# Making the sign words of split weights with a multiply by 0.0 in place of a comparison

## The chip, the cores and the metric

The kernel runs on one core of one Trainium2 chip. The metric is the device time of one execution in microseconds (us), lower is better. Engines are named as the profile names them: PE is TensorE (PEld its weight loads), DVE is VectorE, ACT is ScalarE, POOL is GpSimd, SP issues most of the DMAs.

## What is computed

Causal attention (4 batches, 8 heads, 576 positions, head size 64) with a bias made from running sums of `s`, followed by two dense layers on the 2304 rows of width 512. Each layer goes up to 2048 and back; the first gates with `relu6`, the second with a sigmoid. The weights arrive as 64-bit floating-point numbers.

```python
scores = scale * q @ k.T + min(-(cum[i] - cum[j]), 0), causal
x = softmax(scores) @ v
h = x @ w_in;  x = (h * clip(h + 3, 0, 6) / 6) @ w_out
h = x @ w2_in; out = (h * sigmoid(h)) @ w2_out
```

Only the way in which a weight's 64-bit words become a 32-bit number is touched by the change.

## The kernel before

**Stages.** Up to about 40 us only attention runs, with matmuls on a constant tile (`keep_clock`) between. Up to about 525 us each slot of the program does one head's attention and one step of the first dense layer (`slot`): the step multiplies the weights of one or two chunks with a block of 256 tokens (`first`, L260 to L262), gates the product (`gate_high`: ScalarE L272, VectorE L273, high half `gh` copied on GpSimd by L114), makes the rest `gl` (`gate_low`, VectorE L280), and multiplies by the second weights (`second`, L299 to L301). Every number is carried as a high and a low half, so each product takes three matmuls. Up to about 620 us the last block of 512 tokens runs while the weights of the second layer are prepared, the layer's input is split (`split2`, ScalarE L1033, VectorE L1034 and L1038, names `x1b`, `x1t`, `xr`), and the second layer begins. From there on the second layer has the core to itself (`product` L1068 to L1070, `sums2` L1085 to L1087); the last chunk of weights is prepared before 700 us.

**The feed of weights.** There are 64 chunks of 128 x 512 weights, 16 for each of the four matrices: `i` (up) and `o` (down), for two layers. A chunk goes through `load` (a DMA of 512 KB into a tile `rawi` or `rawo` of 128 x 1024 words, L147), `fields`, `join`, and then, for all but the second layer's up weights, `high` and `low`; those up weights go into sums of a faster product scheme instead (`Two`, L970, L980, L982). In a loaded tile a number's low word and high word lie side by side, so `low` and `high` are every second word of it:

```python
nc.scalar.activation(low, low.bitcast(U32), AF.Copy, scale=2.0**-29)
nc.scalar.activation(f32(self.mag), f32(high), AF.Abs, scale=2.0**-112)
```

The first line (L159) leaves the low word's top three bits as an integer. The second (L160) reads the high word as a 32-bit float and leaves its magnitude, with the exponent moved, in a tile `mag`. L161, on GpSimd, overwrites the high word by its sign alone. `join` on VectorE shifts `mag` left by three and ors the sign word in (L172, two SBUF inputs of integers), then adds the low bits (L176). ScalarE makes the high half of the result (L120), VectorE the low half (L187).

**What sets the order.** `Feed.tick` calls these steps for successive chunks, one chunk a step behind the other; `mag` has three buffers, so L160 of a chunk waits until the chunk three places ahead has been split. The code calls the engines in one order, and then the tile context is opened with `schedule_with_timeline_sim=True`: a planner that holds a duration for every instruction rearranges each engine's stream. A change of an instruction's kind therefore changes the order of others. Within an engine instructions run strictly in that order.

Of the kernel before, what the change touches and what calls it, by code (L numbers as in the profile page):

```python
# [14 lines left out]
ALU = mybir.AluOpType  # L15
# [1 line left out]

P = 128
BIG = 3e38
SIGN = -(2**31)  # L20


def f32(ap):
    return ap.bitcast(F32)
# [3 lines left out]
def kernel(  # L28
# [59 lines left out]
    def heads_of(x):  # L88
# [8 lines left out]
        out=cmask[:, NZ:], in_=cmask[:, NZ:], pattern=[[-1, P]],  # L97
# [32 lines left out]
    class Chunk:  # L130
# [20 lines left out]
        def fields(self):  # L151

            self.mag = stage.tile([P, DM], I32, tag="mag", name=f"mag{self.nm}")
            if self.src.dtype == F32:
                nc.scalar.copy(f32(self.mag), self.val)
                self.val = f32(self.mag)
                return
            low, high = self.words
            nc.scalar.activation(low, low.bitcast(U32), AF.Copy, scale=2.0**-29)  # L159
            nc.scalar.activation(f32(self.mag), f32(high), AF.Abs, scale=2.0**-112)  # L160
            nc.gpsimd.tensor_scalar(  # L161
                out=high, in0=f32(high), scalar1=0.0, scalar2=float(SIGN),
                op0=ALU.is_lt, op1=ALU.mult,
            )

        def join(self):
# [164 lines left out]
    def bank(kind, shape, name):  # L331
# [11 lines left out]
        out=srow, in0=srow, scalar1=0.0, scalar2=1.0 / SCALE, op0=ALU.max, op1=ALU.mult  # L343
# [944 lines left out]
```

## Time and profile before

| what | us |
| --- | --- |
| median of 3 runs | 1000.9 |
| lowest of the runs | 996.92 |
| the profiled execution's own time | 1001.75 |
| its span, first to last instruction | 1000.0 |
| mean granted TensorE clock in it | 0.995 of full |

The rows further down are from that one profiled execution. One of the three runs took 1356.65 us and stands apart from the others. A busy time is the sum over an engine's instructions; a wait is an engine's idle time just before an instruction, put down to what ended it. Times in timelines count from the first instruction.

### The profile page before, as it was taken

What the parts mean: (1) busy time and instruction counts of PE and PEld (TensorE: products, weight loads), DVE (VectorE), ACT (ScalarE), POOL (GpSimd) and SP (SyncE); (2) the same over time, 40 slices, a digit from 0 to 9 for tenths busy, and PEclk for the clock granted to TensorE, in tenths of its full rate; (3) what the DMA queues carried; (4) which work ended last, traced back from release to release, by engine and by line L of the source; (5) the groups of instructions that cost most, each with busy time, mean ns of one, the idle gap of its engine ahead of it and who ended that gap; (6) DMA issues with size and microseconds to landing.
All of it is one profiled execution on the core that took longest, in us unless ns stands there. A gap on an engine that the chain in (4) does not pass through costs nothing.

```text
span 1000.0 us, 17975 instructions
## 1 busy us (share of the span) xinstructions
PE 976.2 (98%) x6292; PEld 895.8 (90%) x6292; DVE 738.4 (74%) x1757; ACT 510.9 (51%) x1177; POOL 311.3 (31%) x323
## 2 busy tenths in 40 slices
PE   8998999999999999999999999999999999999997
PEld 5787989999999999999997877798988989889996
DVE  6898999888789888988877889887574434743343
ACT  6898555554555555555546566564443323432332
POOL 4456743433233443433425465532000000000000
PEclk9999999999999999999999999999999999999999
DMA  5786212312222223213215967434354243442421
GB/s 177 238 273 197 60 34 74 91 44 64 85 69 82 69 57 88 69 53 91 58 31 181 380 239 235 165 117 189 121 205 170 74 147 104 170 156 76 147 74 64
DMA packets 54419, 125.41 MB, mean 125 GB/s; under 512 B 12332, under 2 KB 34076, under 8 KB 51000
## 3 DMA queue, kind: packets, MB, share of 16 engines
q1 hardware_dynamic: 53880, 123.60, 37.3%
q8 instruction: 50, 0.82, 0.3%
q10 hardware_dynamic: 448, 0.66, 0.2%
q14 instruction: 41, 0.34, 0.1%
HBM read 99.52 MB, written 24.69 MB: 124 GB/s over the span
## 4 chain that ended last, share of the span: by engine, by line
PE 75%; DVE 11%; DMA 5%; POOL 3%; issue 2%; ACT 2%; SPq 1%; POOLq 0%; DVEq 0%; ACTq 0%
PE a L1085 6%; PE a L1086 6%; PE a L1087 6%; PE h L1068 5%; PE h L1070 5%; PE h L1069 5%; PE ph L260 5%; PE ph L261 5%; PE ph L262 5%; PE acc L300 4%; PE acc L299 4%; PE acc L301 4%; PE poB L672 4%; POOL rawo L161 2%; PE pt0B L580 1%
## 5 line engine op out<-in xcount | busy, mean ns | idle before, releaser
L300 PE MATMUL acc<-gl,wo 128*128 128x256 f32 (+1 forms) x512 | 152.9, 300 | 3.4 <-DVE gl L280 3.4
L260 PE MATMUL ph<-xh,wi 128*128 128x256 f32 (+1 forms) x512 | 152.9, 300 | 2.5 <-DVE g L273 1.9
L301 PE MATMUL acc<-gh,wo 128*128 128x256 f32 (+1 forms) x512 | 151.5, 297 | 0.0
L261 PE MATMUL ph<-xl,wi 128*128 128x256 f32 (+1 forms) x512 | 150.6, 294 | 0.0
L262 PE MATMUL ph<-xh,wi 128*128 128x256 f32 (+1 forms) x512 | 150.4, 294 | 0.0
L299 PE MATMUL acc<-gh,wo 128*128 128x256 f32 (+1 forms) x512 | 145.3, 300 | 0.0
L1127 ACT ACTIVATE gh<-h 128x384 fp32r<-128x384 f32 x96 | 50.3, 524 | 185.4 <-DVE h L1135 185.3
L1085 PE MATMUL a<-wo,gh 128*128 128x512 f32 x288 | 113.5, 394 | 1.4 <-ACT gh L1127 0.9
L1086 PE MATMUL a<-wo,gh 128*128 128x512 f32 x288 | 113.1, 393 | 0.0
L300 PEld LDWEIGHTS acc<-gl,wo 128*128 128x128 f32 x512 | 98.1, 192 | 8.1 <-DVE gl L280 5.2
L260 PEld LDWEIGHTS ph<-xh,wi 128*128 128x128 f32 x512 | 96.3, 188 | 7.7 <-DVE g L273 3.3
L301 PEld LDWEIGHTS acc<-gh,wo 128*128 128x128 f32 x512 | 98.1, 192 | 3.2
L299 PEld LDWEIGHTS acc<-gh,wo 128*128 128x128 f32 x512 | 96.8, 191 | 3.4
L261 PEld LDWEIGHTS ph<-xl,wi 128*128 128x128 f32 x512 | 96.4, 188 | 3.2
L262 PEld LDWEIGHTS ph<-xh,wi 128*128 128x128 f32 x512 | 96.5, 188 | 3.1
L161 POOL TENSOR_SCALAR rawi<-rawi 128x512 int32<-128x512 f32 x32 | 69.5, 2173 | 80.2 <-ACT magi L160 53.3
L1087 PE MATMUL a<-wo,gl 128*128 128x512 f32 x288 | 90.0, 392 | 0.0
L161 POOL TENSOR_SCALAR rawo<-rawo 128x512 int32<-128x512 f32 x32 | 72.2, 2258 | 49.7 <-ACT mago L160 40.9
L1129 DVE TENSOR_TENSOR gl<-h,gh 128x384 fp32r<-128x384 f32 x96 | 53.8, 560 | 39.8 <-ACT h L1128 38.0
L1135 DVE TENSOR_TENSOR h<-h,u 128x384 f32<-128x384 f32 x72 | 40.1, 557 | 53.5 <-PE h L1070 53.2
L114 POOL TENSOR_SCALAR gh<-g 128x512 fp32r<-128x512 f32 x68 | 49.8, 734 | 88.7 <-DVE g L273 79.6
L1068 PE MATMUL h<-x0t,w 128*128 128x384 f32 x192 | 64.9, 338 | 0.7 <-DVE u L1135 0.7
(221 smaller groups left out, 2564.9 us busy)
## 6 DMA issues: line engine op xcount, KB each, us to landing
w<-w_d SPq DMA_DIRECT2D x18, 1792.0 KB
w_d<-w SPq DMA_DIRECT2D x8, 1792.0 KB
k2B<-in_kT_dram SPq DMA_DIRECT2D x64, 144.0 KB
rawi<-in_w1i_dram SPq DMA_DIRECT2D x16, 512.0 KB
rawo<-in_w1o_dram SPq DMA_DIRECT2D x16, 512.0 KB
rawi<-in_w2i_dram SPq DMA_DIRECT2D x16, 512.0 KB
rawo<-in_w2o_dram SPq DMA_DIRECT2D x16, 512.0 KB
q2B<-in_qT_dram SPq DMA_DIRECT2D x64, 80.0 KB
```

The costliest lines, as they stand in the source:

```text
L161: nc.gpsimd.tensor_scalar(out=high, in0=f32(high), scalar1=0.0, scalar2=float(SIGN), op0=ALU.is_lt, op1=ALU.mult,)
L260: nc.tensor.matmul(o, wih[:, cs], xh[c], start=c == 0, stop=False)
L261: nc.tensor.matmul(o, wih[:, cs], xl[c], start=False, stop=False)
L262: nc.tensor.matmul(o, wil[:, cs], xh[c], start=False, stop=c == NDC - 1)
L299: nc.tensor.matmul(a, woh[:, cs], gh[:, jj, :], start=b0, stop=False)
L300: nc.tensor.matmul(a, woh[:, cs], gl[:, jj, :], start=False, stop=False)
L301: nc.tensor.matmul(a, wol[:, cs], gh[:, jj, :], start=False, stop=b1)
L1068: nc.tensor.matmul(ps, w[:, 0, cs], xh[:, c, :], start=c == 0, stop=False)
L1085: nc.tensor.matmul(accs[t], gh[:, k, cs], woh, start=b0, stop=False)
L1086: nc.tensor.matmul(accs[t], gh[:, k, cs], wol, start=False, stop=False)
L1087: nc.tensor.matmul(accs[t], gl[:, k, cs], woh, start=False, stop=b1)
L1129: nc.vector.tensor_tensor(out=gl[:, i, o], in0=g, in1=f32(gh[:, i, o]), op=ALU.subtract)
```

## The change

The sign word is no longer made by a comparison with 0.0 whose result is multiplied by -2^31 and written as a 32-bit integer. Instead the high word, read as a 32-bit float, is multiplied by 0.0 and by 1.0 and written as a float: the result is 0.0 or -0.0, whose only bit that is ever set is the sign. What `join` reads has the same bits as before. The instruction stays on GpSimd, in place, on the same 512 words a partition, two words apart.

```diff
-SIGN = -(2**31)
...
             nc.gpsimd.tensor_scalar(
-                out=high, in0=f32(high), scalar1=0.0, scalar2=float(SIGN),
-                op0=ALU.is_lt, op1=ALU.mult,
+                out=f32(high), in0=f32(high), scalar1=0.0, scalar2=1.0,
+                op0=ALU.mult, op1=ALU.mult,
             )
```

A line goes from the head of the file, so each line number in the changed kernel is one lower (L161 becomes L160, L114 becomes L113).

The planner gives another order. The first place is GpSimd's stream where the down weights of the second layer begin, near 575 to 610 us of the profile. `rawo_N` is the sign word of chunk N, `gh` the high half of a gated product of the last block; the last number tells tiles apart. Before:

```order
L161 TENSOR_SCALAR rawo_0_8635<-rawo_0_8635 128x512
L114 TENSOR_SCALAR gh_8705<-g_8704 128x512
L161 TENSOR_SCALAR rawo_1_8684<-rawo_1_8684 128x512
L161 TENSOR_SCALAR rawo_2_8723<-rawo_2_8723 128x512
L161 TENSOR_SCALAR rawo_3_8761<-rawo_3_8761 128x512
L114 TENSOR_SCALAR gh_8739<-g_8738 128x512
L161 TENSOR_SCALAR rawo_4_8805<-rawo_4_8805 128x512
L114 TENSOR_SCALAR gh_8781<-g_8780 128x512
L114 TENSOR_SCALAR gh_8821<-g_8820 128x512
L161 TENSOR_SCALAR rawo_5_8848<-rawo_5_8848 128x512
L114 TENSOR_SCALAR gh_8868<-g_8867 128x512
```

Now:

```order
L160 TENSOR_SCALAR rawo_0_8635<-rawo_0_8635 128x512
L160 TENSOR_SCALAR rawo_1_8684<-rawo_1_8684 128x512
L160 TENSOR_SCALAR rawo_2_8723<-rawo_2_8723 128x512
L113 TENSOR_SCALAR gh_8705<-g_8704 128x512
L160 TENSOR_SCALAR rawo_3_8761<-rawo_3_8761 128x512
L113 TENSOR_SCALAR gh_8739<-g_8738 128x512
L160 TENSOR_SCALAR rawo_4_8805<-rawo_4_8805 128x512
L160 TENSOR_SCALAR rawo_5_8848<-rawo_5_8848 128x512
L113 TENSOR_SCALAR gh_8781<-g_8780 128x512
L160 TENSOR_SCALAR rawo_6_8895<-rawo_6_8895 128x512
L113 TENSOR_SCALAR gh_8821<-g_8820 128x512
L113 TENSOR_SCALAR gh_8868<-g_8867 128x512
```

Two more sign words stand ahead of `gh_8705`, one more ahead of `gh_8781`, and one more, `rawo_6`, ahead of `gh_8821`.

The second place is VectorE's stream in the same part of the program. `mago_N` is a chunk's joined words (L172 or L171, and L176 or L175, which is printed as ISA), `wo` its low half, `x1b` the low half of the second layer's input, `s` and `w` the sums of up weights. Before, from the first `x1b` on:

```order
L1034 TENSOR_TENSOR x1b_0_8638<-xr_0_8604,x0b_0_8637 128x768
L970 TENSOR_TENSOR s_8527<-magi_3_8519 128x256
L970 TENSOR_TENSOR s_8527<-magi_2_8515,magi_3_8519 128x256
L172 SCALAR_TENSOR_TENSOR mago_0_8757<-mago_0_8757,rawo_0_8635 128x512
L982 TENSOR_TENSOR w_1_8564<-magi_3_8519,w_1_8564 128x256
L280 TENSOR_TENSOR gl_8706<-g_8704,gh_8705 128x512
L1038 TENSOR_TENSOR xr_0_8604<-xr_0_8604 128x2x384
L970 TENSOR_TENSOR s_8527<-s_8527,magi_2_8515 128x256
L176 ISA mago_0_8757<-rawo_0_8635,mago_0_8757 128x1024
L970 TENSOR_TENSOR s_8527<-magi_2_8515,s_8527 128x256
L172 SCALAR_TENSOR_TENSOR mago_1_8799<-mago_1_8799,rawo_1_8684 128x512
L187 TENSOR_TENSOR wo_0_8839<-mago_0_8757,wo_0_8839 128x512
```

Now, up to the first `x1b` and four rows on:

```order
L171 SCALAR_TENSOR_TENSOR mago_1_8799<-mago_1_8799,rawo_1_8684 128x512
L171 SCALAR_TENSOR_TENSOR mago_2_8841<-mago_2_8841,rawo_2_8723 128x512
L175 ISA mago_1_8799<-rawo_1_8684,mago_1_8799 128x1024
L981 TENSOR_TENSOR w_1_8564<-s_8527,w_1_8564 128x1024
L279 TENSOR_TENSOR gl_8706<-g_8704,gh_8705 128x512
L175 ISA mago_2_8841<-rawo_2_8723,mago_2_8841 128x1024
L171 SCALAR_TENSOR_TENSOR mago_3_8888<-mago_3_8888,rawo_3_8761 128x512
L1033 TENSOR_TENSOR x1b_0_8638<-xr_0_8604,x0b_0_8637 128x768
L186 TENSOR_TENSOR wo_1_8886<-mago_1_8799,wo_1_8886 128x512
L272 SCALAR_TENSOR_TENSOR g_8738<-g_8738,ph_8725 128x512
L175 ISA mago_3_8888<-rawo_3_8761,mago_3_8888 128x1024
L186 TENSOR_TENSOR wo_2_8929<-mago_2_8841,wo_2_8929 128x512
```

The first `x1b` stood ahead of every join of a down chunk; now chunks 0 to 2 are joined ahead of it and chunk 3 is begun.

## Rows read from the trace of the kernel before

**Rows 1.** Page, busy time of the span: us (share) xinstructions, by engine.
```profile
PE 976.2 (98%) x6292; PEld 895.8 (90%) x6292; DVE 738.4 (74%) x1757; ACT 510.9 (51%) x1177; POOL 311.3 (31%) x323
```

**Rows 2.** Stretches: us, busy PE, PEld, DVE, ACT, POOL, granted clock, DMA share.
```profile
0.00:50.00 50.00, 44.57 (x271) 32.67 (x272) 36.37 (x130) 37.22 (x100) 24.34 (x27) 0.97 0.69 208
50.00:150.00 100.00, 92.09 (x718) 87.11 (x717) 95.66 (x242) 72.78 (x173) 59.48 (x41) 0.97 0.45 141
150.00:525.00 375.00, 374.44 (x3068) 369.31 (x3068) 319.07 (x903) 197.33 (x529) 140.17 (x208) 1.00 0.24 68
525.00:600.00 75.00, 74.73 (x321) 59.83 (x320) 61.26 (x91) 46.07 (x76) 41.85 (x26) 1.00 0.74 267
600.00:650.00 50.00, 46.65 (x219) 38.93 (x217) 46.30 (x78) 29.97 (x54) 29.37 (x15) 1.00 0.56 200
650.00:975.00 325.00, 324.14 (x1613) 291.40 (x1612) 171.25 (x299) 121.34 (x234) 16.07 (x8) 1.00 0.37 135
```

**Rows 3.** GpSimd groups: xcount | busy us, mean ns | idle before, releasers.
```profile
L161 POOL TENSOR_SCALAR rawo<-rawo 128x512 int32<-128x512 f32 x32 | 72.2, 2258 | 49.7 <-ACT mago L160 40.9 <-DMA inA<-in_kT_dram 6.9 <-PE h L1070 1.5
L161 POOL TENSOR_SCALAR rawi<-rawi 128x512 int32<-128x512 f32 x32 | 69.5, 2173 | 80.2 <-ACT magi L160 53.3 <-issue 18.6 <-DMA rawo<-in_w1o_dram 4.8
L114 POOL TENSOR_SCALAR gh<-g 128x512 fp32r<-128x512 f32 x68 | 49.8, 734 | 88.7 <-DVE g L273 79.6 <-DVE sums L560 4.1 <-DVE smtB L560 3.1
```

**Rows 4.** Waits in 50 to 150 us: total us, times, longest; TensorE, VectorE.
```profile
PE acc L300 <- DVE gl L280: 2.8, 4, 0.9
PE ph L260 <- DVE g L273: 1.9, 1, 1.9
PE ps0B L517 <- DVE kaB L459: 1.3, 1, 1.3
...
DVE wo L187 <- ACT wo L120: 2.2, 3, 1.0
```

**Rows 5.** VectorE waits in 525 to 650 us: total us, times, longest.
```profile
DVE mago L172 <- POOL rawo L161: 3.8, 2, 1.9
DVE magi L172 <- POOL rawi L161: 3.6, 2, 2.7
```

**Rows 6.** Lines L172, L176: ns min/median/max, first and last start us.
```profile
L172 DVE SCALAR_TENSOR_TENSOR mago<-mago,rawo x32: 664/680/1145, 15.2 to 667.4; 128x512 int32<-128x512 int32 x32
...
L176 DVE CUSTOM_DVE_ANT_0 mago<-rawo,mago x32: 666/680/2429, 17.1 to 668.3; 128x1024 uint16<-128x1024 uint16 x32
```

**Rows 7.** VectorE busy with L172 (first two), L176 (last two), two stretches.
```profile
50.00:150.00 100.00, 16.62 (x23) 0.97 0.45 141
600.00:650.00 50.00, 9.76 (x12) 1.00 0.56 200
...
50.00:150.00 100.00, 18.25 (x24) 0.97 0.45 141
600.00:650.00 50.00, 9.69 (x13) 1.00 0.56 200
```

**Rows 8.** Timeline near 116 us: start us, us, engine, line, op.
```profile
116.51 2.01 POOL L161 TENSOR_SCALAR rawo<-rawo 128x512 int32<-128x512 f32 x1
...
116.73 0.97 DVE L172 SCALAR_TENSOR_TENSOR magi<-magi,rawi 128x512 int32<-128x512 int32 x1
```

**Rows 9.** Timeline near 605 us, GpSimd, VectorE, TensorE: start us, us.
```profile
598.39 0.93 POOL L114 TENSOR_SCALAR gh<-g 128x512 fp32r<-128x512 f32 x1 [0.56 <-DVE g L273]
...
605.46 2.00 POOL L161 TENSOR_SCALAR rawo<-rawo 128x512 int32<-128x512 f32 x1 [2.53 <-ACT mago L160]
...
610.54 2.44 POOL L161 TENSOR_SCALAR rawo<-rawo 128x512 int32<-128x512 f32 x1
...
604.60 0.68 DVE L280 TENSOR_TENSOR gl<-g,gh 128x512 fp32r<-128x512 f32 x1
...
605.33 0.50 PE L300 MATMUL acc<-gl,wo 128*128 128x512 f32 x1 [0.62 <-DVE gl L280]
...
609.28 0.39 PE L300 MATMUL acc<-gl,wo 128*128 128x512 f32 x1
```

## The prediction

> **What bounds the kernel now.** I began with the page's first part [rows 1]: TensorE's matmuls are busy 976.2 of 1000.0 us. GpSimd, where the edited instruction runs, is busy 311.3 us, so its total cannot set the time; only a place where somebody waits for it can. The second view was therefore a table of busy time by stage [rows 2]. It shows two kinds of stage. From 150 to 525 us and from 650 to 975 us TensorE is busy 374.44 of 375 and 324.14 of 325 us: nothing that GpSimd does there can buy more than a microsecond. TensorE has holes in 0 to 50 us (5.43 us), 50 to 150 us (7.91 us) and 600 to 650 us (3.35 us). In 50 to 150 us VectorE is busy 95.66 of 100 us, and in 600 to 650 us 46.30 of 50: there VectorE, not TensorE, is the fullest engine.
>
> Then I asked where the edited line, L161, stands. It runs 64 times, 32 for each kind of weight, for 69.5 + 72.2 = 141.7 us, a mean of 2.21 us [rows 3]. It is the middle of a chain for each weight chunk: ScalarE L159, L160, GpSimd L161, VectorE L172, L176, ScalarE L120, VectorE L187, and then the chunk may be multiplied. Last I read the waits. In 50 to 150 us TensorE waits for VectorE's gates and splits (`gl`, `g`, `kaB`), the longest sum being 2.8 us, and no wait there names L187, L172 or L161: the weights are there before they are wanted. VectorE's own longest wait in that stretch is for ScalarE, 2.2 us [rows 4]. In 525 to 650 us VectorE does wait for L161, 3.8 + 3.6 us in four times [rows 5], while TensorE's holes there are 0.27 us up to 600 and 3.35 us after [rows 2].
>
> **The change part by part.** The edit replaces each of the 64 instructions; no wait, DMA or tile is added. *Its duration.* No row shows a float32 multiply on words that lie two apart. From below it is bounded by the same two multiplies by constants on 512 contiguous elements: L114 `gh`, mean 0.734 us over 68 [rows 3]; a quicker one is not excluded, but little is left under 0.73 us. From above the bound is the smaller of today's two means, 2.17 us, since input and step stay as they are and one operation and a conversion to integers go. Slower than today I exclude, for the multiply is a form that this engine already runs at a third of the time. I take 0.74 us, by the row of L114, which is nearest in operation. So the line falls from 141.7 to 64 x 0.74 = 47.4 us of GpSimd time, 94.3 us less, and each chunk is ready 1.47 us sooner.
>
> [...]
>
> *What lies beside other work.* Nearly all of the 94.3 us. GpSimd is idle before L161 for 80.2 + 49.7 us already, 94.2 us of it for ScalarE's magnitudes [rows 3]; so a shorter L161 mainly makes it wait longer. In 0 to 50 us the ten instructions prepare weights long before the first step uses them; I count 0 there. Cover is gone only if the weights were late, which [rows 4] deny.
>
> *What lies on the path.* First, the shadow that GpSimd throws on VectorE. L172 and L176 have medians of 0.68 us but reach 1.14 and 2.43 us [rows 6]. In 50 to 150 us L172 takes 16.62 us for 23 and L176 18.25 us for 24 [rows 7], which is 16.62 - 15.64 + 18.25 - 16.32 = 2.9 us over the medians; in 600 to 650 us the same reckoning gives 9.76 - 8.16 + 9.69 - 8.84 = 2.45 us. That is 5.4 us of VectorE time in the stretches where VectorE is full. As the time that L161 is running falls to a third, I take two thirds of it back: 3.6 us. The bounds are 0 (the lengthening has another cause) and 5.4; on the other side it may grow, which is a rival below.
>
> [...]
>
> Second, the four waits of 525 to 650 us. Each can shrink by at most 1.47 us, together 5.9 us of VectorE time; but what TensorE can get back is bounded by its holes, 0.27 us before 600 and 3.35 us after [rows 2]. I take a third of the latter, 1.1 us; bounds 0 and 3.4.
>
> *The order.* The program orders instructions by a planner that knows durations, so all engines' streams are reshuffled up to the place where the weights of the second layer are prepared. The work is the same; TensorE's full stages do not care. In the first place shown, GpSimd makes `rawo_1`, `rawo_2` ahead of the high half `gh_8705`, and `rawo_5` ahead of `gh_8781`; in the second, VectorE joins chunks ahead of the split `x1b`. I count 0 for it and price it as a rival.
>
> **The sum.** 3.6 + 1.1 = 4.7 us. The profiled execution took 1001.75 us, of which 1.75 lie around the span of 1000.0; 1001.75 - 4.7 = 997.05 us. It was 0.85 us above the median of the runs shown, 1000.9 us; against that median the forecast is 996.2 us, half a per cent faster. A measurement of this kernel can tell about 2%, 20 us, from no change.
>
> **The rivals.**
> - *Hidden altogether.* The lengthening of L172 and L176 comes from other GpSimd work, and TensorE's holes stay where `gl` and `g` set them. For it: [rows 4] names no weight. Time 1000.9 us, give or take 2.
> - *The feed sets the pace.* Only three magnitudes can be staged, and L161 waits for L160's magnitudes 94.2 us in all [rows 3], so the chain could hold back ScalarE and through it VectorE's queue. Then all of TensorE's 7.91 + 3.35 us of holes come back, and with them slots that are merely thin: 718 matmuls in 100 us stand against 3068 in 375, that is 818 in 100, or 12 us at this pace. Together at most 12 + 3.4 = 15.4 us: 985.5 us. Against it: TensorE never waits on a weight there.
> - *Slower: the high halves queue behind late chunks.* In the profile one `gh` began at 598.39 us and the next chunk's L161 at 605.46 us, held by its magnitude [rows 9]. Now that chunk stands ahead of that `gh`. If the chunk comes no sooner, `gh` starts at 605.46 + 0.74 and takes 0.62, and the difference `gl` takes 0.73 more (604.60 to 605.33): TensorE, which waited until 605.33 us, waits until 607.55, 2.2 us more. The next `gh` then stands behind the chunk of 610.54 us, and its product at 609.28 us would begin at 612.63, 3.35 us late. The delays overlap, so the price is about 3.4 us: 1000.9 + 3.4 = 1004.3 us. It decides if the chunk's magnitude is not at least 5 us earlier than now. Against it: VectorE's joins were brought forward too.
> - *Slower: the shadow gets denser.* If a multiply that finishes in a third of the time blocks VectorE outright, each of the 23 + 12 chunks joined in the full stretches [rows 7] costs one VectorE instruction up to 1.14 - 0.68 = 0.46 us: 16.1 us instead of 5.4, 10.7 us more: 1011.6 us.
> - *The instruction is not quicker.* Then only the new order is left, 1000.9 us within 3.
>
> **Chances.** Forecast 0.48, hidden 0.22, feed 0.12, `gh` behind chunks 0.12, denser shadow 0.04, not quicker 0.02. Faster by over 2% would need 980.9 us or less, below even the feed's case; I leave 0.04 for it. Slower by over 2% would need 1020.9 us; 0.03. Within 2%: 0.93. The range reaches down to the feed's case and up to the queueing of `gh`, 984 to 1006 us; the forecast's own bounds are 1000.9 less 8.8 and less 0, 992 to 1001 us.
>
> **What would show it.** Right: L161's successor at 0.7 to 0.8 us and GpSimd near 217 us busy; VectorE still over 90% busy in 50 to 150 us; TensorE's waits still on `gl`, `g` and the splits; L172 and L176 nearer to 0.68 us in the mean; busy stages of TensorE unchanged. Wrong: a successor over 1.2 us; TensorE's holes in 50 to 150 us gone (then the feed did set the pace); a mean of L172 above 0.76 us (denser shadow); waits on `gl` behind `gh` in the stage near 600 us of over 3 us (queueing).

## The result, and the profile after

The changed kernel took 1007.28 us (median of 6 runs, 1005.05 to 1012.32) against 1001.12 us for the kernel before (median of 6): a ratio of 1.0068 [1.0044, 1.0093], in which the one run of 1356.65 us is left out. I had forecast 996.2 us and a range of 984 to 1006. It is slower, by less than 2%, and 1.3 us beyond my range. The profiled execution is the slowest of the six, 1012.32 us with a span of 1010.5.

The page of the changed kernel, busy time by engine, answers to [rows 1]:

```profile
PE 982.9 (97%) x6292; PEld 900.2 (89%) x6292; DVE 738.9 (73%) x1757; ACT 509.9 (50%) x1177; POOL 226.6 (22%) x323
```

GpSimd fell from 311.3 to 226.6 us, as the instruction's part said. The groups of GpSimd's lines (xcount, busy us, mean ns, idle before and its releasers) answer to [rows 3]:

```profile
L113 POOL TENSOR_SCALAR gh<-g 128x512 fp32r<-128x512 f32 x68 | 53.7, 790 | 120.5 <-DVE g L272 108.1 <-DVE sums L559 4.3 <-DVE smtB L559 3.1
...
L160 POOL TENSOR_SCALAR rawo<-rawo 128x512 f32<-128x512 f32 x32 | 27.1, 849 | 73.4 <-ACT mago L159 72.5 <-DMA rawi<-in_w1i_dram 0.6 <-DMA k2A<-in_kT_dram 0.2
...
L160 POOL TENSOR_SCALAR rawi<-rawi 128x512 f32<-128x512 f32 x32 | 23.2, 727 | 110.7 <-ACT magi L159 66.9 <-PE h L1069 15.2 <-issue 13.8
```

The line that took 141.7 us takes 50.3 (forecast 47.4). So the instruction is three times as quick and the kernel is slower. The table by stretches (us, busy PE, PEld, DVE, ACT, POOL with counts, granted clock, DMA share, GB/s) shows where:

```profile
0.00:50.00 50.00, 44.65 (x233) 32.30 (x234) 32.95 (x116) 32.79 (x89) 9.96 (x25) 0.83 0.72 215
50.00:150.00 100.00, 90.90 (x690) 83.35 (x691) 98.58 (x254) 77.37 (x182) 32.59 (x42) 0.98 0.43 137
...
575.00:650.00 75.00, 69.11 (x306) 56.91 (x305) 71.89 (x109) 46.31 (x79) 26.26 (x26) 0.98 0.64 231
```

The last of these stretches in the kernel before:

```profile
575.00:650.00 75.00, 71.48 (x326) 58.85 (x324) 68.79 (x107) 45.34 (x78) 46.67 (x24) 1.00 0.59 213
```

Between 575 and 650 us TensorE is busy 69.11 of 75 us and runs 306 matmuls; before it was 71.48 us and 326. At the start this one execution ran at a lower granted clock than the one before (0.83 over the first 50 us, 0.97 before). TensorE's waits from 575 to 650 us (total, times, longest) are three, one on each of the engines that feed it:

```profile
PE acc L298 <- POOL gh L113: 2.6, 1, 2.6
PE a L1086 <- DVE gl L1128: 2.3, 1, 2.3
PE a L1084 <- ACT o L119: 1.0, 1, 1.0
```

### The profile page after: what moved, and what is told of

Same layout as the page of the kernel before. It is cut to its first block, busy times and chain, and to the rows that moved or that the text cites. A ratio compares the mean times of both kernels' runs of the same rounds, so it can differ in the third digit from the quotient of the medians.

```text
span 1010.5 us, 17983 instructions
## 1 busy us (share of the span) xinstructions
PE 982.9 (97%) x6292; PEld 900.2 (89%) x6292; DVE 738.9 (73%) x1757; ACT 509.9 (50%) x1177; POOL 226.6 (22%) x323
## 4 chain that ended last, share of the span: by engine, by line
PE 74%; DVE 11%; DMA 6%; issue 4%; ACT 2%; SPq 2%; POOL 2%; POOLq 0%; DVEq 0%; ACTq 0%
PE a L1084 6%; PE a L1086 6%; PE a L1085 6%; PE h L1067 5%; PE h L1068 5%; PE h L1069 5%; PE acc L299 5%; PE acc L298 5%; PE acc L300 5%; PE ph L259 5%; PE ph L260 4%; PE ph L261 4%; PE poB L671 3%; DMA rawi<-in_w2i_dram 2%; PE pt0B L579 1%
## 5 line engine op out<-in xcount | busy, mean ns | idle before, releaser
L1126 ACT ACTIVATE gh<-h 128x384 fp32r<-128x384 f32 x96 | 50.3, 524 | 193.5 <-DVE h L1134 193.4
L1086 PE MATMUL a<-wo,gl 128*128 128x512 f32 x288 | 90.4, 393 | 2.3 <-DVE gl L1128 2.3
L113 POOL TENSOR_SCALAR gh<-g 128x512 fp32r<-128x512 f32 x68 | 53.7, 790 | 120.5 <-DVE g L272 108.1
L279 DVE TENSOR_TENSOR gl<-g,gh 128x512 fp32r<-128x512 f32 (+1 forms) x76 | 55.8, 734 | 14.7 <-POOL gh L113 14.5
L1068 PE MATMUL h<-x1t,w 128*128 128x384 f32 x192 | 64.8, 338 | 0.0
```

Of the source, the lines that this page charges most:

```text
L279: nc.vector.tensor_tensor(out=gl, in0=g, in1=f32(gh), op=ALU.subtract)
L1068: nc.tensor.matmul(ps, w[:, 0, cs], xl[:, c, :], start=False, stop=False)
L1086: nc.tensor.matmul(accs[t], gl[:, k, cs], woh, start=False, stop=b1)
```

## The experiments

All times are medians; each ratio is against runs of the kernel before on the same chip in the same session. The changed kernel was timed in its own session alone, so where its 1007.28 us stands beside an experiment's time, two sessions are compared.

| kernel | us (runs) | ratio to before |
| --- | --- | --- |
| E1 comparison, order planned for the multiply | 1033.32 (5) | 1.0312 [1.0284, 1.0341] |
| E2 multiply, order planned for the comparison | 996.24 (12) | 0.9955 [0.9935, 0.9974] |
| E3 multiply, second layer's order new | 1006.54 (12) | 1.0039 [1.0018, 1.0061] |
| E4 multiply, first layer's order new | 998.78 (12) | 0.9977 [0.9959, 0.9995] |
| E5 changed kernel, gate moved on VectorE | 1005.98 (12) | 1.0062 [1.0038, 1.0086] |
| E6 changed kernel, second-layer gate moved | 1006.29 (12) | 1.0056 [1.0035, 1.0077] |
| E7 both | 1006.39 (12) | 1.0047 [1.0031, 1.0064] |
| E9 planner told of up chunks and four down | 1001.42 (12) | 0.9997 [0.9978, 1.0016] |
| E10 told of the down chunks | 1000.14 (12) | 0.9987 [0.9973, 1.0001] |
| E11 told of the up chunks | 999.77 (12) | 0.9981 [0.9963, 0.9999] |
| E12 changed kernel, sums behind products | 1008.03 (8) | 1.0046 [1.0028, 1.0064] |
| E13 E7 and E12 | 1006.25 (12) | 1.0050 [1.0031, 1.0068] |
| E14 E13 and a copy moved on ScalarE | 1007.17 (10) | 1.0044 [1.0027, 1.0061] |
| E15 changed kernel, VectorE's rest ahead of chunks | 1016.74 (5) | 1.0158 [1.0130, 1.0186] |

E8 and E16 measure instructions by themselves and have no ratio.

**E1 and E2: the instruction apart from the order.** The program is built with one form, so that the planner orders it for that form; then all 64 instructions are replaced, in place, by the other form.

```diff
     with _tile.TileContext(nc, schedule_with_timeline_sim=True) as tc:
         tile_attention_moe_moe_kernel(tc, *args)
+    put_sign(nc, "old")   # E1: built with the multiply, runs the comparison
+    put_sign(nc, "new")   # E2: built with the comparison, runs the multiply
```

> The comparison on GpSimd (2.2 us each), every engine's stream in the order of the changed kernel. If the new order is what costs, this is as slow as the changed kernel or a little slower: 1006 to 1013 us, with TensorE at the lower clock for over 10 us before 45 us. If the multiply itself is what costs (a denser shadow on VectorE), the loss is gone: 999 to 1003 us.

> The multiply on GpSimd, every engine's stream in the order of the kernel before. If the new order is what costs, this is not slower than before and shows what the quicker instruction is worth by itself: 995 to 1001 us (my forecast of 4.7 us less would be 996). If the multiply itself costs, 1005 to 1009 us.

E2 is 996.24 us, which is the number I had forecast for the changed kernel. With the changed kernel (multiply, new order) and the one before (comparison, old order) this is a square: the instruction alone gains 1001.12 - 996.24 = 4.9 us; the new order alone costs 1007.28 - 996.24 = 11.0 us with the quick instruction (11.3 by the two ratios) and 1033.32 - 1001.12 = 32.2 us with the slow one. E1 lies 20 us above what I expected of either case: over its whole execution VectorE waits 32.0 us for sign words, where the kernel before has 8.3 and the changed kernel 12.4. E2 is also the version that beats both kernels. In its stretch from 575 to 650 us TensorE loses almost nothing; the stretch from 50 to 150 us is discussed with the prediction:

```profile
50.00:150.00 100.00, 91.26 (x737) 86.33 (x736) 96.31 (x250) 73.07 (x174) 33.80 (x42) 1.00 0.43 140
...
575.00:650.00 75.00, 74.24 (x351) 63.77 (x351) 69.38 (x112) 48.41 (x84) 26.54 (x22) 1.00 0.53 184
```

Its joins on VectorE (groups of lines; the mean is the number behind the busy time) show the shadow term:

```profile
L172 DVE SCALAR_TENSOR_TENSOR magi<-magi,rawi 128x512 int32<-128x512 int32 x32 | 24.1, 754 | 1.5 <-POOL rawi L161 1.5
L172 DVE SCALAR_TENSOR_TENSOR mago<-mago,rawo 128x512 int32<-128x512 int32 x32 | 22.9, 714 | 1.1 <-POOL rawo L161 1.1
L176 DVE CUSTOM_DVE_ANT_0 mago<-rawo,mago 128x1024 uint16<-128x1024 uint16 x32 | 23.1, 721 | 0.1
L176 DVE CUSTOM_DVE_ANT_0 magi<-rawi,magi 128x1024 uint16<-128x1024 uint16 x32 | 22.9, 714 | 0.1
```

Together 93.0 us; the same four groups take 25.1 + 23.4 + 24.7 + 23.0 = 96.2 us before, so 3.2 us came back (forecast 3.6). VectorE's waits for the sign words fell from 7.4 us [rows 5] to 2.6 in the same stretch.

**E3 and E4: which layer's order.** As E2, but the planner is told of the multiply for one layer's chunks only; every sign word is made by the multiply in both.

```diff
+            if self.key[1] == 0:      # E3: a chunk of the first layer; E4: == 1
+                nc.gpsimd.tensor_scalar(
+                    out=high, in0=f32(high), scalar1=0.0, scalar2=float(SIGN),
+                    op0=ALU.is_lt, op1=ALU.mult,
+                )
+            else:
+                nc.gpsimd.tensor_scalar(
+                    out=f32(high), in0=f32(high), scalar1=0.0, scalar2=1.0,
+                    op0=ALU.mult, op1=ALU.mult,
+                )
...
+    put_sign(nc, "new")
```

> The multiply everywhere; the planner was told of it for the second layer's chunks alone, so that the streams differ from before only from about 500 us on. If the loss comes from the opening (TensorE's clock, first step 5.2 us late, 8.8 us late by the end of the first layer's feed), this run has none of it: 995 to 1001 us. If it comes from the high halves queued behind sign words near 600 us, this has it: 2 to 5 us over the run with the old order.

> The multiply everywhere; the planner was told of it for the first layer's chunks alone, so that the streams are those of the changed kernel up to about 500 us and near those of before from there. If the loss comes from the opening, it is all here: 1004 to 1010 us, first dense step at about 45 us. If it comes from the stage near 600 us, 995 to 1002 us.

The second layer's order costs 1006.54 - 996.24 = 10.3 us, the first layer's 2.5; together 12.8 against the 11.0 of the whole. E3 came out at twice the 2 to 5 us that I had expected over E2. So by the medians the opening is the smaller part: E4 has the changed kernel's opening and is the second best of all. E3 runs the same instructions as E2 in the same order up to some 525 us, and behind that it stops keeping up. Its rows, and below them E4's from 50 to 150 us:

```profile
0.00:50.00 50.00, 43.65 (x247) 31.67 (x248) 34.14 (x122) 34.96 (x94) 10.26 (x26) 0.91 0.67 205
...
575.00:650.00 75.00, 69.51 (x306) 58.11 (x305) 71.66 (x110) 47.38 (x83) 25.39 (x25) 0.95 0.57 204
```

```profile
50.00:150.00 100.00, 89.69 (x704) 82.82 (x704) 97.49 (x253) 74.38 (x180) 37.32 (x45) 1.00 0.45 145
```

From 575 to 650 us E3 runs 306 matmuls where E2 runs 351, with TensorE idle for 5.5 us where E2's is for 0.8, and a granted clock of 0.95. Its waits are those of the changed kernel: 2.3 us on `gh`, 2.3 on `gl`, 0.9 on `o`. Slices of 5 us of E3 (columns as above) show what follows each of the two longer ones, and how full VectorE is:

```profile
590.00:595.00 5.00, 4.27 (x19) 3.11 (x17) 5.00 (x8) 5.00 (x10) 2.65 (x1) 1.00 0.97 361
595.00:600.00 5.00, 3.46 (x10) 2.79 (x11) 4.49 (x6) 1.35 (x3) 4.08 (x4) 0.76 0.06 22
600.00:605.00 5.00, 5.00 (x21) 3.94 (x20) 5.00 (x8) 3.17 (x5) 1.97 (x2) 0.90 0.00 0
605.00:610.00 5.00, 5.00 (x25) 4.23 (x24) 5.00 (x8) 3.47 (x6) 0.62 (x1) 1.00 0.79 264
...
630.00:635.00 5.00, 3.26 (x8) 2.53 (x9) 5.00 (x10) 3.69 (x8) 0.71 (x1) 0.68 0.81 304
```

In the slice of TensorE's hole the granted clock is 0.76 and in the next one 0.90; the slice of the other hole has 0.68. Of the changed kernel's two long waits the one of 2.6 us, over at 601.95 us, came with 0.68 in 600 to 605 us: from 602 to 605 us the granted clock is 0.50, and matmuls of 128x512 begin 0.43 us apart where they began 0.23 us apart before the wait. So this wait cost more than its own length. The one of 2.3 us came with 1.00 in every slice from 630 to 650 us. Over whole executions E3's granted clock has a median of 0.990 where E2's is 0.9945, and E3's fastest run (1000.21 us) is the one at 0.998, its slowest (1009.09) the one at 0.984. If a mean clock lower by 0.0045 costs that share of 1000 us, it is 4.5 of E3's 10.3 us, and by the same reckoning (0.991) 3.5 of the changed kernel's 11.0; the idle time itself is 5.5 - 0.8 = 4.7 us of E3's. The two make 9.2 of the 10.3.

The traces place the loss. The matmuls counted from the start, when the 4300th begins and how long it is from there to the 4600th, by which the second layer has TensorE to itself:

| kernel | clock, first 50 us | 4300th matmul, us | to the 4600th, us |
| --- | --- | --- | --- |
| before | 0.97 | 583.0 | 69.2 |
| E2 | 1.00 | 578.3 | 64.9 |
| E3 | 0.91 | 585.5 | 72.8 |
| E4 | 1.00 | 583.4 | 64.9 |
| changed | 0.83 | 590.6 | 72.0 |

The second layer's order costs 7 to 8 us in its beginning (E3 against E2, changed against E4). E3's other 7 us over E2 arise in the opening, where the two have the same order: there this one execution ran at a granted clock of 0.91 for the first 50 us, E2's at 1.00. E4 against E2 is the first layer's order at the same clock (0.999 over both executions): 5.1 us, with 704 matmuls from 50 to 150 us where E2 has 737. The medians, 2.5 us apart, may hide half of that: E4's runs have a median clock of 0.997 where E2's have 0.9945. So the first layer's order is worth 2.5 to 5 us and is not a trifle.

**E5 to E7: two of the waits taken away.** The wait on `gh` has a cause that the timeline shows. GpSimd of the changed kernel, 595 to 605 us (start, us, engine, line):

```profile
597.76 4.13 POOL L113 TENSOR_SCALAR gh<-g 128x512 fp32r<-128x512 f32 x1 [5.71 <-DVE g L272]
601.86 1.70 POOL L160 TENSOR_SCALAR rawo<-rawo 128x512 f32<-128x512 f32 x2
603.79 0.92 POOL L113 TENSOR_SCALAR gh<-g 128x512 fp32r<-128x512 f32 x1 [0.23 <-DVE g L272]
```

and VectorE at the same time:

```profile
597.53 0.68 DVE L175 CUSTOM_DVE_ANT_0 mago<-rawo,mago 128x1024 uint16<-128x1024 uint16 x1
598.13 0.68 DVE L186 TENSOR_TENSOR wo<-mago,wo 128x512 fp32r<-128x512 f32 x1
598.73 0.94 DVE L1037 TENSOR_TENSOR xr<-xr 128x768 f32<-128x768 f32 x1
599.60 1.81 DVE L1033 TENSOR_TENSOR x1b<-xr,x0b 128x768 fp32r<-128x768 f32 x2
601.92 1.11 DVE L279 TENSOR_TENSOR gl<-g,gh 128x512 fp32r<-128x512 f32 x1 [0.51 <-POOL gh L113]
```

A `gh` of 4.13 us, where the mean of the 68 is 0.79; it was over at 601.89 us, 0.48 us after VectorE's row. E1 and E3 have it too, and E6 and E9 below: 4.13 us each time (begun at 607.17, 592.35, 591.62 and 588.04 us), beside the same five instructions of VectorE. In the moves, VectorE's instruction that reads the first name goes ahead of the one that writes the second, and the counts that others wait for follow:

```diff
     with _tile.TileContext(nc, schedule_with_timeline_sim=True) as tc:
         tile_attention_moe_moe_kernel(tc, *args)
+    move_up(nc, "_8739", "2_8929")    # E5, E7: gl of gh_8739 ahead of wo, xr, x1b, x1b
+    move_up(nc, "_9013", "10_9253")   # E6, E7: gl of h_9013 ahead of two joins' steps
```

> The changed kernel, every instruction and every engine's order as it is but one: on VectorE the low half gl that reads the high half gh_8739 stands directly behind the join of chunk 3, ahead of the row wo, xr, x1b, x1b that it stood behind. Theory (a queue in front of the new order's gates): in the changed kernel that gh took 4.13 us on GpSimd, 597.76 to 601.89, exactly as long as VectorE ran wo, xr, x1b and x1b without a gap, TensorE waited 2.6 us for it and then ran 3.4 us at half clock. With VectorE waiting for the gh in place of running those four, the gh takes under 1 us, TensorE's wait and the half clock behind it go: 2.6 + 1.7 = 4.3 us, 1007.3 becomes 1003.0 (1001.5 to 1004.5), at a cost of up to 0.7 us of VectorE's idle time. Rival (VectorE is simply full there): the x1b come 1.3 us later and TensorE waits for those or for the next gl in place of this one; the time stays within 1 us of 1007.3. Rival (the clock at the start makes the loss): no change either, and a mean clock under 0.99 as before.

> The changed kernel with one other move on VectorE: the low half gl of the second layer's first gates that reads h_9013 stands ahead of the add of chunk 10, four instructions earlier. Theory: TensorE waited 2.3 us for it at 637.1, while its input h was ready from ScalarE at 634.0; VectorE had two joins and two adds of weight chunks ahead of it. The wait falls to some 0.2 us: 1007.3 becomes 1005.2 (1003.5 to 1006), or some 1.7 us lower in executions that ran at half clock behind that wait. Rival (full VectorE): the chunks 10 to 12 come late instead, TensorE waits for weights wo near 640 us, the time stays within 1 us.

> The changed kernel with both moves. Theory: the gains add, 4.3 + 2.1 = 6.4 us, 8 with the clock: 1000.9 (999 to 1002); what is then left above the 996.24 us of the multiply in the old order are some 2.5 us of the first layer's new order and 1.0 us of a wait on ScalarE's o at 631 us. Rival (full VectorE): 1005.5 to 1008.5 with the waits moved on. If the gains do not add, the second wait was the first one's echo or the other way round.

The moves did what they should: in E5 and E7 that `gh` takes 0.93 and 0.94 us, and the waits on `gh` and on L1086's `gl` are gone. The time is not: 1005.98, 1006.29 and 1006.39 us, at most 1.3 us under the changed kernel (2.1 by the ratios, inside their intervals). That is nearest to the rival in each; E5 and E6 fall just between the two ranges. TensorE's waits of E7, 575 to 660 us, show where the gain went:

```profile
PE a L1084 <- ACT o L119: 3.7, 1, 3.7
PE acc L299 <- DVE gl L279: 0.5, 1, 0.5
PE h L1067 <- DVE g L272: 0.3, 1, 0.3
PE h L1067 <- DVE h L1134: 0.2, 1, 0.2
```

The third wait, 1.0 us behind the two others, is 3.7 us without them, and the granted clock is 0.50 from 625 to 630 us, behind it. TensorE reaches it earlier, and `o` comes when it came: the first sum begins 40.7 us behind the 4300th matmul in the changed kernel and 40.8 us behind it in E7.

**E8: GpSimd beside VectorE.** Leaves the whole computation out.

```diff
+    for v in (None, v_sub, v_join, v_add, v_one):      # eight VectorE instructions without a gap
+        for p in (None, p_sign, p_copy, p_cmp):        # one of GpSimd, begun inside them
```

> Leaves the whole computation out: GpSimd's multiply two words apart, its contiguous copy and the old comparison, each alone and each begun inside a chain of eight VectorE instructions without gaps: subtractions of two float32 inputs 128x768 (as x1b), joins (shift and or, the second input two words apart), adds of the low words, and copies with one input. Theory (a VectorE chain with two SBUF inputs stops GpSimd as long as it has no gap): alone 0.65 to 0.75, 0.62 and 2.0 to 2.2 us; beside subtractions the multiply and the copy end only when the chain does, 4 to 7 us; beside joins and adds the same; beside one-input copies up to 1 us. Rival (as my prediction had it, an instruction of one engine delays the other by no more than one instruction): nowhere over 1.9 us for multiply and copy, and VectorE's instructions are the ones that grow.

The rival holds. One line's instructions (min/median/max ns; alone is the minimum):

```profile
L63 POOL TENSOR_SCALAR rawo<-rawo x10: 655/953/1198, 13.9 to 281.7; 128x512 f32<-128x512 f32 x10
L66 POOL TENSOR_SCALAR rawo<-rawo x10: 1987/2276/2537, 22.4 to 294.8; 128x512 int32<-128x512 f32 x10
L69 POOL TENSOR_SCALAR gh<-g x10: 617/855/918, 17.6 to 287.7; 128x512 f32<-128x512 f32 x10
L72 DVE TENSOR_TENSOR z<-x,y x64: 942/948/1389, 25.5 to 211.6; 128x768 f32<-128x768 f32 x64
L81 DVE COPY z<-x x64: 407/420/861, 127.9 to 296.0; 128x512 f32<-128x512 f32 x64
```

L63 is the multiply, L66 the comparison, L69 the contiguous copy. None of them is kept out until a chain's end (at most 1.20, 2.54 and 0.92 us), and one VectorE instruction of the chain grows by some 0.43 us: eight subtractions take 7.04 us alone and 7.47 beside the multiply, and the longest `z` of L81 took 0.86 us against a median of 0.42. Which of the three ran beside a chain made no difference there: eight copies with one input took 3.21, 3.19 and 3.21 us beside the multiply, the contiguous copy and the comparison, eight joins 5.32 and 5.34 beside the last two.

**E9 to E11: how much of the plan is new.** If no single wait makes the loss, it may be the plan's common feature: chunks that seem ready sooner are joined ahead of the gates, splits and copies that TensorE waits for. In VectorE's order 16 instructions of down or late up chunks stand ahead of the last split `x1t` in E2, 25 in E3. Telling the planner of the multiply for some chunks gives values between.

```diff
-            if self.key[1] == 0:                                    # E3
+            if not (self.key[:2] == ('i', 1) or self.key[:2] == ('o', 1) and self.key[2] < 4):   # E9
+            if not (self.key[:2] == ('o', 1)):                      # E10
+            if not (self.key[:2] == ('i', 1)):                      # E11
```

> The multiply in all 64 places, as in the replanned second layer; but the planner knows of it only for that layer's up chunks and the first four down chunks. VectorE's order then has 24 instructions of weight chunks ahead of the last split x1t of the layer's input, as against 16 in the old order and 25 in the fully replanned one; TensorE's order keeps the 12 matmuls of products between its last acc of the first layer and its first sum a, which the fully replanned order has lost. Theory (backlog: chunks that seem ready sooner are joined ahead of what TensorE waits for, each at some 0.65 us or more on a VectorE that is full there): by the two known orders, 16 for 996.2 and 25 for 1006.5 us, one chunk instruction ahead costs 1.14 us, so 1005.4 (1003.5 to 1007). Rival (TensorE's own order: without products between, each sum a waits for the copies of acc): 997 (995.5 to 999).

> The same with the planner told for the second layer's down chunks alone: 20 chunk instructions ahead of the last x1t, TensorE's 12 product matmuls in place. Theory (backlog): 996.2 + 4 x 1.14 = 1000.8 (999 to 1002.5). Rival (TensorE's order): 997 (995.5 to 999).

> The same with the planner told for the second layer's up chunks alone: 19 chunk instructions ahead of the last x1t, TensorE's 12 product matmuls in place. Theory (backlog): 996.2 + 3 x 1.14 = 999.7 (998 to 1001.5). Rival (TensorE's order): 997 (995.5 to 999).

E10 and E11 fall where the backlog puts them (1000.14 for 1000.8, 999.77 for 999.7) and against the rival's 997. E9 does not: with 24 chunk instructions ahead it takes 1001.42, 4 us under the line and 4.4 over the rival. So the loss grows with the part of the plan that is new, by some 3.5 to 5 us, but the count of chunk instructions ahead doesn't carry the last 5 us between E9 and E3 (4.2 by the ratios). The clock may: the median granted clock is 0.996 over E9's runs and 0.990 over E3's, by the reckoning above 6 us. E9 also has the `gh` of 4.13 us, which by itself is therefore not worth what E3 loses.

**E12 to E14: the last wait.** E3 differs from E9 also in that its first sums `a` follow the last `acc` directly, with no products between.

```diff
+    move_up(nc, "_8739", "2_8929")                        # E13, E14
+    move_up(nc, "_9013", "10_9253")                       # E13, E14
+    move_down(nc, "PE", "_9165", 3, ("_9137",))           # E12 to E14: 3 sums behind 12 products
+    move_down(nc, "Activation", "_8951<-_8999", 1, ("_9048",))   # E14: four steps behind the copy
+    move_down(nc, "Activation", "_9381", 1, ("_9048",))
+    move_down(nc, "Activation", "o1_9_9379", 1, ("_9048",))
+    move_down(nc, "Activation", "o1_14_9388", 1, ("_9048",))
```

The product that now stands first took over the sums' wait for VectorE (0.8 us in E12, for VectorE's `o`), because VectorE's add of the product before reads the bank that it writes.

> The changed kernel with one move on TensorE: the first three sums a_2 of the second layer stand behind the 12 product matmuls that followed them (2.1 us of work), as in the old order, so that ScalarE's copy o of the accumulator they reuse is covered. In the changed kernel's profile that wait was only 1.0 us, behind two longer ones. Theory (the waits are in a row, and the last of them shows only what the earlier ones have not already spent): 1006.3 (1005 to 1007.3). Rival (the lost cover is the cause by itself, and makes the 5 us between the order that kept it, 1001.4, and the one that did not, 1006.5): 1002.5 (1001 to 1004).

> Both VectorE moves and the TensorE move. With the VectorE moves alone TensorE waited 3.7 us for o at 621.5 and ran on at half clock. Theory (a row of waits): now 2.1 us of that are covered: 1006.4 - 2.1 - up to 1.7 = 1003.5 (1002 to 1005). Rival (VectorE's backlog passes every gain on to the next wait): 1005.5 to 1007.

> The three moves, and on ScalarE the copy o_2 goes ahead of the two chunk steps, the cast wo and the gate gh that stood between o_0 and it. Theory (a row of waits, this the last): the 3.7 us and the half clock behind them are gone: 1006.4 - 3.7 - 1.7 = 1001.0 (999.5 to 1002.5), which is where the orders with the backlog but with TensorE's cover lie (999.8 to 1001.4), plus the first layer's new order. Rival (VectorE's backlog passes every gain on): 1004 to 1007, with the wait on a gate gl or a product.

E13 and E14, 1006.25 and 1007.17 us, are the rival's case (E14 0.2 us above its range). E12 is not: its rival, the lost cover as the cause by itself, wanted 1002.5 us, and 1008.03 us is 0.7 above even the theory's range. So the lost cover by itself makes none of the loss. TensorE's longest wait of E14 is nearly as long as E7's, on another engine and another instruction:

```profile
PE h L1067 <- DVE o L121: 3.6, 1, 3.6
PE acc L299 <- DVE gl L279: 0.5, 1, 0.5
```

VectorE of E14, which has no gap from 590 us to there but 0.5 us:

```profile
620.95 0.68 DVE L186 TENSOR_TENSOR wo<-mago,wo 128x512 fp32r<-128x512 f32 x1
621.55 0.55 DVE L1134 TENSOR_TENSOR u<-h,u 128x384 f32<-128x384 f32 x1
622.02 0.68 DVE L175 CUSTOM_DVE_ANT_0 mago<-rawo,mago 128x1024 uint16<-128x1024 uint16 x1
622.62 1.12 DVE L186 TENSOR_TENSOR wo<-mago,wo 128x512 fp32r<-128x512 f32 x1
623.66 0.55 DVE L1134 TENSOR_TENSOR h<-h,u 128x384 f32<-128x384 f32 x1
624.13 0.54 DVE L1134 TENSOR_TENSOR u<-h,u 128x384 f32<-128x384 f32 x1
624.59 0.68 DVE L121 COPY o<-acc 128x512 f32<-128x512 f32 x1
```

The product's own need is the last add `u`, over at 624.67; the copy `o` behind it adds 0.6 us. TensorE had been ready since 621.7. In the row stand three steps of weight chunks that no wait of TensorE names, ahead of adds that TensorE needs.

**E15: VectorE's order alone.** The changed kernel with 46 of VectorE's 96 instructions between 583 and 648 us put earlier, ahead of steps of chunks, wherever the trace showed that their inputs had been there before that step ended.

```diff
+    reorder(nc, 1142, [0, 1, 2, 4, 5, 6, 7, 9, 3, 8, 10, 11, 12, 14, 15, 18, 13, 20, 23, 16, 17,
...
```

> The changed kernel with VectorE's order alone changed, between 583 and 648 us of its profile: every gate, split, sum, add and copy goes ahead of the steps of weight chunks that it stood behind, wherever its inputs were there before that step had ended in the changed kernel's trace; all other engines as they are. Theory (VectorE's backlog of chunk steps is what TensorE waits for, in whichever place it shows): the waits on gh, gl and o near 600 and 631 to 637 us shrink together, 1007.3 becomes 1001 (999 to 1003). Rival (VectorE has no slack in this stage whatever the order, the chunks then come late in their turn; or TensorE's own new order is what loses): 1005 to 1007.5.

Neither: 1016.74 us, 9.5 us more than the changed kernel. TensorE's three longest waits from 575 to 660 us and, below, VectorE's two:

```profile
PE a L1084 <- ACT mago L159: 4.0, 1, 4.0
PE acc L299 <- DVE gl L279: 2.5, 1, 2.5
PE a L1084 <- ACT gh L1126: 1.3, 1, 1.3
```

```profile
DVE g L272 <- ACT g L271: 4.0, 4, 1.9
DVE gl L1128 <- ACT h L1127: 3.1, 3, 1.7
```

ScalarE's queue and GpSimd's still have the chunks early. A chunk's cast on ScalarE now waits for a join that VectorE does later, and the gates and copies behind that cast wait with it: from 575 to 660 us ScalarE's casts wait 20.7 us for joins, against 9.0 in the changed kernel. The four engines' orders were planned together, and putting VectorE's right alone made it worse here.

**E16: what held the `gh` of 4.13 us.** Leaves the whole computation out: chains of the very kinds that ran beside it.

```diff
+    for busy in (False, True):                         # ScalarE idle, or casting
+        for v in (v_wo, v_xr, v_x1, v_seq):            # eight VectorE instructions; gh begun inside
```

> Leaves the whole computation out: GpSimd's copy gh begun inside chains of eight VectorE instructions of the kinds that ran beside the gh of 4.13 us, low halves wo, differences xr, splits x1, and a mixture of the three, with ScalarE idle and with ScalarE casting. Theory A (one of these kinds shuts GpSimd out from instruction to instruction, as the plain subtractions of the earlier look did not): a gh of 3 us or more beside that kind. Theory B (VectorE's instruction lets GpSimd in at its end, as in the earlier look): 0.85 to 1.2 us beside every kind with two inputs, and what held the gh of 4.13 us is something else, such as ScalarE's casts of the same tiles (then over 2 us only with ScalarE busy).

Theory B, and its second half fails: the 15 copies that began inside a chain took 0.82 to 1.38 us, the same with ScalarE idle and busy (1.21 beside the splits and 1.38 beside the mixture in both; one more, beside no chain, took 0.62). One of them inside seven splits without a gap:

```profile
29.15 6.57 DVE L72 TENSOR_TENSOR x<-xr,x 128x768 fp32r<-128x768 f32 x7
29.36 1.21 POOL L62 TENSOR_SCALAR gh<-g 128x512 fp32r<-128x512 f32 x1 [7.43 <-ACT g L59]
```

What held the other one for 4.13 us stays open. The traces have more of its kind: in E11 a `gh` took 3.53 us, and in the changed kernel another one, begun at 104.30 us, took 2.80. All three ended 0.47 to 0.49 us after the last of four or five VectorE instructions without a gap, nearly all with two inputs in SBUF, which was over at 594.36, 106.61 and 601.41 us. That is what the theory of E8 said; but in E8 and E16 no such row kept GpSimd out (at most 1.20 us for the multiply, 1.38 for the copy).

## Why the prediction was wrong

*What bounds the kernel* held: TensorE, with holes in three stretches, and VectorE next to full in 50 to 150 us (98.58 of 100) and near 600 us (5.00 in each 5 us from 605 to 645).

*The duration* held: 0.73 and 0.85 us against 0.74 forecast, 50.3 us against 47.4. (The reason for the upper bound was loose: both forms have two operations; a multiply stands in place of the comparison. No run shows the 1.2 us that I set as the limit.)

*The shadow* held in size as VectorE's time in the old order (3.2 us of joins in E2 against 3.6), and not in its reason. I took two thirds back because the multiply runs for a third of the time. E8 shows that VectorE's chain grows alike beside either form (eight copies took 3.21 us beside the multiply and beside the comparison). In the changed kernel, with its other order, the joins' shadow hardly fell (95.7 us for the four groups, against 96.2): L171 has a mean of 0.77 us, just over the 0.76 that I had named as a sign of a denser shadow, where E2's L172 has 0.73.

*The four waits* held in direction and were priced too low: VectorE waits 4.8 us less for sign words in E2, and TensorE's idle time from 575 to 650 us fell from 3.5 to 0.8 us, 2.7 us where I took 1.1.

*The sum* held for what it described, by luck to this digit. E2 is the change without the new order: 996.24 us for 996.2, with an interval of some 2 us to each side. The traces put the gain elsewhere: from the 4300th to the 4600th matmul E2 needs 4.3 us less than the kernel before, where my terms give 2.7 (1.1 for the waits and two thirds of 2.45 for the shadow). In 50 to 150 us I counted 1.9, but TensorE's holes there did not shrink (8.7 us in E2, 7.9 before); E2's lead of 4.7 us up to the 4300th matmul comes with a granted clock of 1.00 in the first 150 us against 0.97.

*The order* is the step that failed: "The work is the same; TensorE's full stages do not care ... I count 0 for it". It costs 11.0 us, shown by the square of E1, E2 and the two kernels. The larger part, 10.3 us in E3's median and 7 to 8 us in the traces, is the second layer's beginning, where TensorE is not full and three engines feed it by turns; the first layer's order makes 2.5 to 5 us. By the reckoning with the mean clock less than half of E3's loss (4.5 us) is time at a lower clock, which I had not priced at all. I had both places of that order before me and priced one of them, at 3.4 us and a chance of 0.12.

*The queueing rival* came nearest (1004.3) and is not what the trace shows. It wanted `gh` held behind a sign word whose magnitude was late. The `gh` of 597.76 us began when its own input `g` came; it ran long. My sign for it, a wait of over 3 us, was not reached by any single wait (2.6 us).

*The range* ended at 1006 because I added up one wait. What the changed order does looks like a backlog: three waits, each of which only uncovers the next (E5 to E7, E12 to E14). The price of this order wasn't the longest wait that one could name; it was four times that. The range should have held several.

What is shown: the loss is the order's; the second layer's part is the larger one; it grows with the part that is planned anew (E11, E10, E9, E3; the step from E9 to E3 may be the clock's); none of the moves of one, two or four kinds that were tried takes it away; the reordering of VectorE alone that was tried doesn't either. What is argued only: that the chunks' steps, put early on all four engines because they seem ready sooner, are the backlog. A program that puts them back on all four at once is E2, which agrees, but changes everything else of the order too.

## What to carry to other kernels

Where a planner orders the program from instruction durations, a quicker instruction is two changes: the instruction, and a new order for everything near it. Build the one without the other before judging either; here they were -4.9 and +11.0 us, and the change without its order is the best of all the kernels timed. A wait that several engines share was not removed here by moves on one engine, nor by a few on three: before pricing such a wait, ask who is late next, and keep that in the range.

## What the runs showed of the hardware

- The same 512 words, two apart: 0.66 us for the multiply with a float32 result, 1.99 us for the comparison with an integer result, both alone (E8); 0.62 us for the multiply of contiguous words. The step of two words costs 0.04 us here, the comparison or the conversion (which of them was not tried apart) 1.3 us.
- In E8 a GpSimd instruction begun inside a chain of VectorE instructions lengthens one of them by some 0.43 us (7.47 us for eight subtractions beside the multiply, 7.04 alone), the same beside one of 0.66 us and one of 1.99 us (3.21 us for eight copies beside either), and also where VectorE's have a single input (0.42 to 0.86 us). In the kernel before a `L172` begun inside a `L161` was over 0.82 us before it [rows 8]. Where GpSimd is let in can only be estimated: the eight subtractions are 0.87 us apart (7.04 us alone, 0.94 for the last), so the second one beside the multiply ends at about 36.33 + 2 x 0.87 = 38.07 us; the multiply, begun inside it at 37.47, was over at 38.67, 0.60 us later, close to the 0.66 us that it takes alone; so its work began at about the end of the one running. GpSimd's own instruction is longer there too: 0.66 us alone and at most 1.20 for the multiply, 0.62 and at most 0.92 for the copy (E8), at most 1.38 for the copy in E16.
- Yet in five programs (E1, E3, E6, E9 and the changed kernel) a copy of that kind took 4.13 us beside five VectorE instructions, and neither E8 nor E16 reproduces it.
- With the slow instruction, the order planned for the quick one costs 32.2 us, three times as much as with the quick one: in this kernel an order whose planned durations weren't kept lost far more than the 4.9 us that the instruction itself is worth.
- Two waits of 2.3 us of TensorE came with slices of 5 us at a granted clock of 0.68 to 0.90 (E3, 595 to 605 and 630 to 635 us); a wait of the same length in the changed kernel, over at 637.14 us, came with 1.00, its wait of 2.6 us, over at 601.95 us, with 0.50 from 602 to 605 us.
